# The fourth group's odd half of the out-projection by seven products, in a gated scan with two feed-forward layers

## The chip, the cores and the metric

One core of a Trainium2 chip runs the whole program. The metric is the device time of one execution in microseconds (us). The engines are TensorE (PE in the profile), VectorE (DVE), ScalarE (ACT), GpSimd (POOL) and SyncE (SP), whose queue issues the DMAs. Products on TensorE go to PSUM banks; all else lies in SBUF or in DRAM.

## The reference, cut to what matters

```python
f = lower_bound + (1.0 - lower_bound) * sigmoid(f_logit)      # 6080 x 256
h = f[t] * h + (1.0 - f[t]) * x[t]                            # for t in range(6080)
h1 = y @ moe_w_in;   g1 = maximum(0.01 * h1, h1);             x2 = g1 @ moe_w_out
h2 = x2 @ moe2_w_in; g2 = where(h2 > 0, h2, exp(minimum(h2, 0)) - 1)
return g2 @ moe2_w_out                                        # 6080 x 256, w_in 256 x 2048
```

A scan over 6080 tokens gives `y` (one row `h` per token), and two feed-forward layers of width 2048 follow, the first with a leaky gate, the second with an exponential one.

## The kernel before, in words

**Tiling.** The tokens are cut into 12 chunks: 512, then 448, then ten of 512. The width 2048 is cut into four groups (q = 0 to 3) of 512. `stream` (from line 292) lists the work as 96 triples (layer, chunk, group): layer 1's chunks 0 and 1 alternate inside each group, then chunks 2 to 11 follow with four groups each, then layer 2's twelve chunks. Each triple has an inward part (256 inputs to 512 hidden values) and an outward part (back to 256 outputs, summed over the four groups of a chunk in PSUM).

**Three matmuls a product.** Numbers are kept as a high and a low part that TensorE can take. `mm3` (line 672; its matmuls are L678, L679 and L680) multiplies high by high, high by low and low by high, in pieces of 256 columns, or of 448 in the short chunk.

**Seven products.** From chunk 2 on, the inward part splits both matrices in two by two blocks and does seven products instead of eight (`product` in `group`), with sums and differences of blocks made beforehand: of the chunk by `operands` (L511, L517, L524), of the weights by `combine` (L328). The outward part has an even half (rows E) and an odd half (rows O) of the gate's values. The even half is always plain: `straight`. The odd half is plain as well, or goes by seven products where `seven(l, c, q)` says so; the table `SEVEN` (line 215) holds that for each layer and group as a range of chunks. For such a group `odd_operands` (line 956) makes the differences on VectorE (L969 one of 512 columns, L966 two of 256), casts to a high part on ScalarE (L980: 768 and 1024 columns) and makes the low part on VectorE (L983, the same sizes), into two operand tiles, `aB` and `aT`. A plain half has one cast (L857) and one low part (L861) of 1024 columns. Out of the seven products three go straight to banks 1 and 0 of the chunk (`some(gates["B"], ...)`), and four (`some(gates["T"], ...)`, the group's last) to bank 0 and to two extra banks, `s` and `z`. At the end of a chunk `leave` (line 991) copies `s` and `z` out with ScalarE (L1029), adds them up on VectorE (L1031, L1032, L1036) and adds the sums to banks 1 and 0 (L1033, L1041).

**Weights.** `weights` (line 362) decodes one unit of weights on VectorE and ScalarE (L416, L419, L422, L425, L429) and splits it in high and low. Units that go by seven products (`sums`) are stored as seven blocks. In layer 1 such an odd unit first stays plain, and `finish` (line 338; L349, L328, L355, L357) turns it into seven blocks after the last chunk that uses it plain. The sixteen units of layer 2 are prepared while layer 1 runs, one about every two groups from the 17th triple on, are stored in DRAM (`w2d`) and fetched by `reload` (line 461) when layer 1 needs its weights no more. Where a group of layer 2 goes back to plain, `back` loads the one block that the plain form needs again.

**What sets the order.** All operations are first collected by a planner (`Plan`): each has an engine, a cost in us, a due time, operations that it comes after, and tiles that it takes and gives from pools (seven PSUM banks and one seed bank, six operand tiles, five `h`, three `ws`, and so on). `emit` then fills the engines' queues: of the operations that could start, that with the lowest rank is next, where a rank is the due time of the users less the costs on the way. Each engine runs its queue in order. `SHIFT` holds for each kind of group a string of letters that move ranks by steps of a quarter of a us (N is none). So `SHIFT`, and the costs, change only the order of the instructions and which tile each takes.

Of the kernel before, what the change touches and what calls it, by code (L numbers as in the profile page):

```python
# [15 lines left out]
ALU = mybir.AluOpType  # L16
P = 128
SHIFT = {
    (1, 'x', 0): 'NNNNNNNNNNNNNNNNN7',
    (1, 'w', 'I2'): 'NrNNBN?',  # L20
    (1, 'w', 'O2'): 'NNiUXe',
    (1, 'w', 'E0'): 'NMNNNm',
    (1, 'x', 1): 'NNNNi.9NNNNNNONFNNNkg4',
    (1, 0, 'first1'): 'N*NNNNNNNNNNNNNNNNNNNNN*',
    (1, 1, 'first0'): 'NNNNN*NNNNNN7',
    (1, 1, 'first1'): 'NNNNNNNNNNNNNNNNNNNNN4',
    (1, 'f', 'I'): 'N_eNPbANX',
    (1, 2, 'first0'): 'NNNNNNNNNNNNNNNN2',
    (1, 2, 'first1'): '*',
    (1, 'w', 'O0'): 'NNN1Nir',  # L30
    (1, 3, 'first0'): 'NNNNNNNNNNNN^NN*NNNNNNNNr',
    (1, 3, 'first1'): 'NNNNNNNNNNNNfJNNNNNNNNN;NNNc',
    (1, 'x', 2): 'NNNNANNNNN5UV8NNNNN*NNNN\\NNr@N`=Na*SKNq',
    (1, 0, False): 'NNNNNNNNNNNNNNNNNa6',
    (1, 1, False): 'NNN-NNNN5NNNNNNNaNMN*',
    (1, 'f', 'O'): 'NNNNN8I',
    (1, 2, False): 'NNNNNNNNlNNNNNNNNf',
    (1, 3, False): 'NNN3NENNLNNNN6:YN+RNNNNNN/NNNNNNNN6',
    (1, 0, True): 'N>NNNHNNKNNNNN?NNVNkNNNNNNNNN1',
    (1, 1, True): 'NNNNNNNNNNUNNDNNAN2KBNNNrN1NN5',  # L40
    (1, 2, True): 'NNNNNNNNNN>NNNlNNNNNcNN1R',
    (2, 'w', 'I2'): '-rcNNZH01r=N+_NI',
    (2, 'w', 'O2'): 'NNNNNNNN*NNNNNNr',
    (2, 'w', 'E0'): 'N]NENp',
    (2, 'x'): 'NNNNNNNYR',
    (2, 0, True): 'NWNLNMNNNN*NNJN5NNa[<L>lNN:NNKNNNNNA',
    (2, 1, True): 'NNNrNNNNNNNNNNENNNNNNN<TN>NNEP',
    (2, 2, True): 'NNNNNNNN<NNNN*T=NNNNRMBgIiNNELNNNNN*',
    (2, 3, False): 'NNN<NNNNNN;NNN2NNS5ENN1rNNNNNNNNNNNN7NNN\\NNNN8NNNB',
    (2, 0, 'last'): 'NNNANNNNNNNNN<=5NNNNSNNNNNNNNN+',  # L50
    (2, 1, 'last'): 'NNNNNNNNFNNNNNNNNNNNNNNNNNNNN/',
    (2, 2, 'last'): 'NN,NNNNNNNNNNNNYN:HiYN/',
    (2, 3, 'last'): 'NNNNNNNNNNNNNNCSNnNNNNNXQ5NNNNNNNNNNNNNNNNNNN<',
}


# [103 lines left out]
def kernel(  # L160
# [51 lines left out]


    SI, SO = 7 * P, 2 * D
    SEVEN = {(1, 0): range(3, 12), (1, 1): range(3, 12), (1, 2): range(3, 12), (2, 0): range(0, 11), (2, 1): range(0, 11), (2, 2): range(0, 11)}

    def sums(l, u):

# [39 lines left out]
    def v2(n):  # L258
        return 0.07 + n / 1920.0

    def s1(n):
        return 0.09 + n / 1200.0

    def mm(n):
        return max(0.111, n * 0.000444)
# [8 lines left out]
    def dve(*a, **k):  # L274
        return plan.add("DVE", *a, **k)
# [86 lines left out]
    def weights(l, u, due, gate=()):  # L362
# [46 lines left out]
        def val():  # L409
# [6 lines left out]
        up = dve(v2(n), None, lambda: nc.vector.tensor_scalar(  # L416
            out=tile_("up"), in0=top(), scalar1=0x7F, scalar2=None, op0=ALU.bitwise_and,
        ), [ld], take=[(b, "up", "up")])
        sg = dve(v2(n) + 0.05, None, lambda: nc.vector.tensor_scalar(  # L419
            out=fr(), in0=top().bitcast(I8), scalar1=2.0, scalar2=-2.0, op0=ALU.min, op1=ALU.max,  # L420
        ), [ld], take=[(b, "wf", "ws")])
        ex = act(s1(n) + 0.1, None, lambda: nc.scalar.activation(  # L422
# [156 lines left out]
    def gated(c, natural, gates, hold):  # L579
# [8 lines left out]
        for k in range(KD):  # L588
# [6 lines left out]
            for nm, src in (("f", f2), ("x", x2)):  # L595
                if natural:
                    def load(nm=nm, src=src, k=k, b=b):
                        nc.sync.dma_start(
                            out=b["r" + nm][2][:pb, : n // pb * P].rearrange("p (b d) -> p b d", d=P),
                            in_=src[t0 : t0 + n, k * P : (k + 1) * P].rearrange("(b p) d -> p b d", p=pb),  # L600
                        )

                    ld = dma(0.75 if c == 0 and k else 0.9, (-200.0 + 4 * k if nm == "f" else -199.0 + 5 * k) if c == 0 else None, load, gates[:1], take=[(b, "r" + nm, "raw")], late=3.1)

                    def turn(nm=nm, b=b, k=k):
                        for i in range(n // pb):
# [80 lines left out]
    def group(i):  # L687
# [36 lines left out]
            return o  # L724

        def snap(name, bank, after):
            return act(s1(2 * h), None, lambda: nc.scalar.copy(out=ps(name), in_=ps(bank)), after, take=[(b, name, "sn")])  # L727

        def add(name, s, bank, sn, after, **k):
            return dve(v1(2 * h), None, lambda: nc.vector.tensor_tensor(  # L730
# [30 lines left out]
            gO, gE = "hO", "hE"  # L761
        else:
            pX = product("X", A11, B11, True, False, [], take=[(b, "X", "bank"), (b, "R", "bank")])
            z1 = act(s1(2 * h), None, lambda: nc.scalar.copy(out=ps("Y"), in_=ps("X")), [pX], take=[(b, "Y", "seed")])
# [12 lines left out]
            if final:  # L777
                pass
            elif l == 1:
                a, o = (act(s1(2 * h), None, lambda s=s, name=name: nc.scalar.activation(  # L780
                    out=half("hO", s), in_=two(ps(name)), func=AF.Prelu, alpha=0.01), [done],
                    take=[(b, "hO", "h")], give=[(b, name, home)])
                    for s, name, done, home in ((1, "Y", C11, "seed"), (0, "X", pX, "bank")))
# [3 lines left out]
                gO, gE = "hO", "hE"  # L787
            else:

                a, o = (act(s1(2 * h), None, lambda s=s, name=name: nc.scalar.activation(  # L790
                    out=half("eO", s), in_=two(ps(name)), func=AF.Relu, scale=-1.0), [done],
                    take=[(b, "eO", "ws")])
                    for s, name, done in ((1, "Y", C11), (0, "X", pX)))
# [197 lines left out]
    def leave(l, c, i, yb, swapped):  # L991
# [30 lines left out]
        if "s" in last:  # L1022
# [3 lines left out]
            def at(s, e=None):  # L1026
                return sb["sb"][2][:, s * h : (e or s + 1) * h]

            cps = [act(s1(n), soon, lambda s=s, k=k: nc.scalar.copy(out=at(s, s + 2), in_=yb[k][2][:, :n]), [last[k]],  # L1029
                       take=[(sb, "sb", "h")], give=[(yb, k, "bank")]) for s, k in ((0, "s"), (2, "z"))]  # L1030
            u2 = dve(v1(h), soon, lambda: nc.vector.tensor_tensor(out=at(2), in0=at(2), in1=at(1), op=ALU.add), cps)  # L1031
            u4 = dve(v1(h), soon, lambda: nc.vector.tensor_tensor(out=at(0), in0=at(0), in1=at(2), op=ALU.add), [u2])  # L1032
# [19 lines left out]
            return  # L1052
        for k in (1, 0):
            tb = {}
            tr = dve(v1(n), None, lambda tb=tb, k=k: nc.vector.transpose(
                out=tb["o"][2][:, :n], in_=(ob[k]["o"] if done else yb[k])[2][:, :n]),
                [done.get(k), last[k]], take=[(tb, "o", "t")], give=[(ob[k], "o", pool_) if done else (yb, k, "bank")])
            sent = []
# [89 lines left out]
```

## Time and profile before

| | us |
|---|---|
| median of 3 runs | 981.82 (981.72 to 981.86) |
| the profiled execution | 981.77 |
| its span, first to last instruction | 979.7 |
| ScalarE busy | 812.8 (83 % of the span) |
| GpSimd busy | 14.8 (2 %) |
| TensorE's granted clock | 1.000 of full speed, mean |

The busy time of an engine is the time in which an instruction of it was recorded; matmuls are pipelined and their ends are modelled. The share of the chain that ended last is 97 % TensorE, 1 % VectorE, and under half a per cent for ScalarE and for DMAs.

### The profile page before, as it was taken

To read this page: it belongs to the slowest core of one execution; us is meant where nothing else is said; L and a number is where in the kernel's file an instruction comes from. 1 tells how busy PE (TensorE), PEld (TensorE's weight loads), DVE (VectorE), ACT (ScalarE), POOL (GpSimd) and SP (SyncE) were. 2 spreads that over 40 slices of the span, in tenths; PEclk is the share of its full clock that TensorE was granted. 3 is DMA by queue.
4 is the path that set the end of the run, shared out by engine and by line. 5 is a ranking of instruction groups with operands and counts; after the bars stand their busy time and mean duration, and the time that the engine had idled before them with its cause. 6 is when DMAs were issued, how large, how long until landed. Compare 5 with 4: busy or idle time off the path is not lost.

```text
span 979.7 us, 20612 instructions
## 1 busy us (share of the span) xinstructions
PE 972.4 (99%) x8330; PEld 967.0 (99%) x8330; DVE 889.4 (91%) x1376; ACT 812.8 (83%) x1202; POOL 14.8 (2%) x22
## 2 busy tenths in 40 slices
PE   8999999999999999999999999999999999999998
PEld 8999999999999999999999999999999999999998
DVE  7899999999999899897689889999999999999975
ACT  6767787898888979888689798888898888988874
POOL 0000000000000000000000000000000000000000
PEclk9999999999999999999999999999999999999999
DMA  6542314556466465535860101012011020110210
GB/s 197 131 118 56 77 41 114 128 120 160 110 145 132 109 156 128 124 107 166 282 230 30 23 22 42 14 31 40 13 37 23 23 45 11 34 23 22 39 23 22
DMA packets 162702, 81.98 MB, mean 84 GB/s; under 512 B 133808, under 2 KB 148400, under 8 KB 162608
## 3 DMA queue, kind: packets, MB, share of 16 engines
q1 hardware_dynamic: 160032, 74.12, 28.4%
q0 software_dynamic: 2304, 6.55, 4.7%
q8 instruction: 65, 1.06, 0.5%
q14 instruction: 29, 0.24, 0.1%
q10 hardware_dynamic: 272, 0.00, 0.0%
HBM read 48.54 MB, written 32.11 MB: 82 GB/s over the span
## 4 chain that ended last, share of the span: by engine, by line
PE 97%; DVE 1%; DMA 0%; ACT 0%; issue 0%; DVEq 0%
PE bank L679 30%; PE bank L678 30%; PE bank L680 30%; PE bank L903 2%; PE seed L678 2%; PE seed L680 2%; PE seed L679 2%; DMA raw<-in_f_logit_dram 0%; DVE bt L645 0%; DVE ws L425 0%; DVE t L637 0%; DVE ws L429 0%; DVE wI L444 0%; PE bank L607 0%; DVE up L416 0%
## 5 line engine op out<-in xcount | busy, mean ns | idle before, releaser
L679 PE MATMUL bank<-op,wI 128*128 128x256 f32 (+2 forms) x1136 | 316.8, 279 | 0.8 <-DVE op L556 0.8
L678 PE MATMUL bank<-op,wI 128*128 128x256 f32 (+2 forms) x1136 | 316.7, 279 | 0.0
L680 PE MATMUL bank<-op,wI 128*128 128x256 f32 (+2 forms) x1136 | 316.4, 279 | 0.0
L679 PEld LDWEIGHTS bank<-op,wI 128*128 128x128 f32 x1136 | 213.4, 188 | 2.1 <-DVE op L556 1.6
L678 PEld LDWEIGHTS bank<-op,wI 128*128 128x128 f32 x1136 | 213.4, 188 | 1.0 <-DVE h L730 0.2
L680 PEld LDWEIGHTS bank<-op,wI 128*128 128x128 f32 x1136 | 213.4, 188 | 0.6 <-DVE wI L444 0.2
L679 PE MATMUL bank<-op,wE 128*128 128x256 f32 (+1 forms) x704 | 197.2, 280 | 0.0
L678 PE MATMUL bank<-op,wE 128*128 128x256 f32 (+1 forms) x704 | 197.2, 280 | 0.0
L680 PE MATMUL bank<-op,wE 128*128 128x256 f32 (+1 forms) x704 | 197.1, 280 | 0.0
L679 PE MATMUL bank<-op,wO 128*128 128x256 f32 (+2 forms) x656 | 182.9, 279 | 0.0
L678 PE MATMUL bank<-op,wO 128*128 128x256 f32 (+2 forms) x656 | 182.8, 279 | 0.0
L680 PE MATMUL bank<-op,wO 128*128 128x256 f32 (+2 forms) x656 | 182.7, 279 | 0.0
L730 DVE TENSOR_TENSOR h<-bank,sn 128x512 f32<-128x512 f32 (+1 forms) x176 | 119.5, 684 | 28.5 <-PE bank L680 23.8
L680 PEld LDWEIGHTS bank<-op,wE 128*128 128x128 f32 x704 | 132.2, 188 | 0.4
L678 PEld LDWEIGHTS bank<-op,wE 128*128 128x128 f32 x704 | 132.2, 188 | 0.4
L679 PEld LDWEIGHTS bank<-op,wE 128*128 128x128 f32 x704 | 132.2, 188 | 0.3
L678 PEld LDWEIGHTS bank<-op,wO 128*128 128x128 f32 x656 | 123.2, 188 | 0.3
L680 PEld LDWEIGHTS bank<-op,wO 128*128 128x128 f32 x656 | 123.2, 188 | 0.2
L679 PEld LDWEIGHTS bank<-op,wO 128*128 128x128 f32 x656 | 123.2, 188 | 0.2
L727 ACT COPY sn<-bank 128x512 f32<-128x512 f32 (+1 forms) x176 | 102.3, 583 | 10.5 <-PE bank L680 9.7
L983 DVE TENSOR_TENSOR op<-h,op 128x768 fp32r<-128x768 f32 (+2 forms) x87 | 98.1, 1131 | 5.8 <-ACT op L980 5.7
L980 ACT CAST op<-h 128x768 fp32r<-128x768 f32 (+2 forms) x87 | 85.3, 981 | 19.9 <-PE bank L680 18.3
(115 smaller groups left out, 1828.5 us busy)
## 6 DMA issues: line engine op xcount, KB each, us to landing
ws<-in_moe_w_in_dram SPq DMA_DIRECT2D x32, 255.6 KB, 3.7
ws<-in_moe_w_out_dram SPq DMA_DIRECT2D x32, 255.6 KB, 3.5
w2dI<-ws SPq DMA_DIRECT2D x16, 448.0 KB, 2.8
wI<-w2dI SPq DMA_DIRECT2D x8, 896.0 KB, 6.9
y1d<-t SPq DMA_DIRECT2D x22, 256.0 KB, 2.9
bt<-y1d SPq DMA_DIRECT2D x22, 256.0 KB, 2.9
raw<-in_f_logit_dram SPq DMA_DIRECT2D x80, 64.0 KB, 2.9
raw<-in_x_dram SPq DMA_DIRECT2D x80, 64.0 KB, 2.5
```

What stands on the lines that cost most here:

```text
L678: nc.tensor.matmul(ps[:, s], wop[0], a[0][:, s], start=start and z == 0, stop=False, skip_group_check=True)
L679: nc.tensor.matmul(ps[:, s], wop[0], a[1][:, s], start=False, stop=False, skip_group_check=True)
L680: nc.tensor.matmul(ps[:, s], wop[1], a[0][:, s], start=False, stop=stop, skip_group_check=True)
L727: return act(s1(2 * h), None, lambda: nc.scalar.copy(out=ps(name), in_=ps(bank)), after, take=[(b, name, "sn")])
L730: return dve(v1(2 * h), None, lambda: nc.vector.tensor_tensor(out=half(name, s), in0=two(ps(bank)), in1=two(ps(sn)), op=ALU.add), after, **k)
L903: nc.tensor.matmul(dst, ops(part, j, t), wide(z, j), start=s in fresh and t % 2 + j + z == 0, stop=False, skip_group_check=True)
L980: hi = act(s1((e - s) * h), None, lambda s=s, e=e, src=src: nc.scalar.copy(out=part(0, s, e), in_=src()), [*after, *highs[-1:]], take=[(b, ...
L983: lows.append(dve(v1((e - s) * h), None, lambda s=s, e=e, src=src: nc.vector.tensor_tensor(out=part(1, s, e), in0=src(), in1=part(0, s, e) ...
```

## The change

The table `SEVEN` gets two more entries: the fourth group's odd half goes by seven products in layer 1 from chunk 3 on, and in layer 2 in chunks 0 to 5. By `sums` the fourth odd unit is then kept as seven blocks in both layers (its SBUF tile grows from 2 x 512 to 2 x 896 values a partition), layer 1 finishes it after chunk 2, and layer 2 reloads its plain block before chunk 6. Some costs that the planner counts with are set anew: ScalarE's copies out of PSUM 0.03 us less (`s1p`), VectorE's transposes 0.025 more, one decoding step 0.05 less. All strings of `SHIFT` are replaced.

```diff
 SHIFT = {
-    (1, 'x', 0): 'NNNNNNNNNNNNNNNNN7',
...
-    (2, 'w', 'I2'): '-rcNNZH01r=N+_NI',
...
+    (1, 'x', 0): 'NNNNNNNNNNNNNNN8',
...
+    (2, 'w', 'I2'): 'NWNrfgRNF6IN+NNT',
...
-    SEVEN = {(1, 0): range(3, 12), (1, 1): range(3, 12), (1, 2): range(3, 12), (2, 0): range(0, 11), (2, 1): range(0, 11), (2, 2): range(0, 11)}
+    SEVEN = {(1, 0): range(3, 12), (1, 1): range(3, 12), (1, 2): range(3, 12), (1, 3): range(3, 12), (2, 0): range(0, 11), (2, 1): range(0, 11), (2, 2): range(0, 11), (2, 3): range(0, 6)}
...
+    def s1p(n):
+        return 0.06 + n / 1200.0
...
-        sg = dve(v2(n) + 0.05, None, lambda: nc.vector.tensor_scalar(
+        sg = dve(v2(n), None, lambda: nc.vector.tensor_scalar(
...
-                    got[nm] = dve(v1(n), None, lambda nm=nm, tl=tl: nc.vector.transpose(out=tl(nm), in_=tl("r" + nm)),
+                    got[nm] = dve(v1(n) + 0.025, None, lambda nm=nm, tl=tl: nc.vector.transpose(out=tl(nm), in_=tl("r" + nm)),
...
-            return act(s1(2 * h), None, lambda: nc.scalar.copy(out=ps(name), in_=ps(bank)), after, take=[(b, name, "sn")])
+            return act(s1p(2 * h), None, lambda: nc.scalar.copy(out=ps(name), in_=ps(bank)), after, take=[(b, name, "sn")])
```

The other lines that are left out put `s1p` for `s1` at four more copies out of PSUM, and the 0.025 at the transpose of the output.

## Rows read from the trace of the kernel before

**Rows 1.** The page: busy us, share of the span, instructions of an engine

```profile
PE 972.4 (99%) x8330; PEld 967.0 (99%) x8330; DVE 889.4 (91%) x1376; ACT 812.8 (83%) x1202; POOL 14.8 (2%) x22
```

**Rows 2.** TensorE in order of time: start us, us, what

```profile
653.51 0.28 PE L678 MATMUL bank<-op,wO 128*128 128x256 f32 x1
...
654.87 0.28 PE L678 MATMUL bank<-op,wI 128*128 128x256 f32 x1
```

**Rows 3.** Busy time by stretch: stretch, us, busy us and instructions, clock, DMA share, GB/s

```profile
120.00:440.00 320.00, 320.00 (x2826) 320.00 (x2825) 305.59 (x501) 274.55 (x421) 12.36 (x14) 1.00 0.52 121
440.00:520.00 80.00, 80.00 (x709) 80.00 (x708) 63.66 (x92) 63.61 (x93) 1.73 (x2) 1.00 0.63 212
520.00:600.00 80.00, 80.00 (x661) 78.94 (x660) 72.01 (x107) 68.24 (x99) 0.00 (x0) 1.00 0.13 27
644.50:684.30 39.80, 39.80 (x353) 39.80 (x353) 37.55 (x54) 34.88 (x50) 0.00 (x0) 1.00 0.13 28
```

**Rows 4.** TensorE's waits: who waited for whom, us, times, longest us

```profile
PE bank L679 <- DVE op L556: 0.8, 2, 0.5
```

**Rows 5.** TensorE in order of time, in the chunk of 448 tokens

```profile
566.32 0.27 PE L678 MATMUL bank<-op,wO 128*128 128x224 f32 x1
...
567.65 0.29 PE L678 MATMUL bank<-op,wI 128*128 128x256 f32 x1
```

**Rows 6.** VectorE in order of time, in a layer-2 chunk

```profile
657.21 0.69 DVE L969 TENSOR_TENSOR h<-ws 128x512 f32<-128x512 f32 x1
657.81 0.42 DVE L1031 TENSOR_TENSOR h<-h 128x256 f32<-128x256 f32 x1
658.15 0.42 DVE L966 TENSOR_TENSOR h<-ws,h 128x256 f32<-128x256 f32 x1
...
660.50 0.95 DVE L983 TENSOR_TENSOR op<-ws,op 128x768 fp32r<-128x768 f32 x1
661.37 1.22 DVE L983 TENSOR_TENSOR op<-h,op 128x1024 fp32r<-128x1024 f32 x1
```

**Rows 7.** VectorE's groups, 120 to 440 us: busy us, mean ns, idle us before

```profile
L730 DVE TENSOR_TENSOR h<-bank,sn 128x512 f32<-128x512 f32 x65 | 44.5, 686 | 11.7 <-PE bank L680 11.1 <-ACT h L785 0.2
...
L328 DVE TENSOR_TENSOR ws<-ws 128x128 f32<-128x128 f32 x44 | 11.2, 284 | 0.1
...
L425 DVE SCALAR_TENSOR_TENSOR ws<-ws,ws 128x512 int32<-128x512 int32 x15 | 10.2, 682 | 0.0
...
L419 DVE TENSOR_SCALAR ws<-ws 128x512 f32<-128x512 int8 x15 | 6.6, 439 | 0.0
...
L328 DVE TENSOR_TENSOR h<-h 128x128 f32<-128x128 f32 x12 | 3.2, 283 | 0.0
...
L349 DVE TENSOR_TENSOR h<-wO 128x512 f32<-128x512 f32 x3 | 2.0, 665 | 0.0
L357 DVE TENSOR_TENSOR wO<-h,wO 128x384 fp32r<-128x384 f32 x3 | 1.6, 548 | 0.0
L357 DVE TENSOR_TENSOR wO<-h,wO 128x128 fp32r<-128x128 f32 x3 | 0.8, 278 | 0.0
```

**Rows 8.** ScalarE in order of time, in the same layer-2 chunk

```profile
656.23 1.08 ACT L1029 COPY h<-bank 128x512 f32<-128x512 f32 x2
...
658.27 0.84 ACT L980 CAST op<-ws 128x768 fp32r<-128x768 f32 x1
```

**Rows 9.** DMA issues: count, KB each, median us from issue to landing

```profile
wO<-w2dO SPq DMA_DIRECT2D x6, 128.0 KB, 3.9
```

**Rows 10.** TensorE in order of time, where the next chunk's outward products begin

```profile
669.15 0.28 PE L678 MATMUL bank<-op,wO 128*128 128x256 f32 x1
```

**Rows 11.** VectorE's groups in a layer-2 chunk, 644.5 to 684.3 us

```profile
L861 DVE TENSOR_TENSOR op<-ws,op 128x1024 fp32r<-128x1024 f32 x5 | 6.1, 1219 | 0.5 <-ACT op L857 0.5
...
L805 DVE SCALAR_TENSOR_TENSOR ws<-ws,h 128x1024 f32<-128x1024 f32 x4 | 4.9, 1222 | 1.2 <-ACT ws L803 1.2
...
L796 DVE SCALAR_TENSOR_TENSOR ws<-ws,seed 128x512 f32<-128x512 f32 x4 | 2.7, 686 | 0.4 <-ACT ws L794 0.2
```

More of the change, by code (lines that the diff above doesn't have):

```diff
@@ L18 @@
 SHIFT = {
-    (1, 'x', 0): 'NNNNNNNNNNNNNNNNN7',
[L20 to L41, printed above, removed]
-    (2, 'w', 'I2'): '-rcNNZH01r=N+_NI',
@@ L43 @@
[L43 to L52, printed above, removed]
@@ L53 @@
-    (2, 3, 'last'): 'NNNNNNNNNNNNNNCSNnNNNNNXQ5NNNNNNNNNNNNNNNNNNN<',
+    (1, 'x', 0): 'NNNNNNNNNNNNNNN8',
+    (1, 'w', 'I2'): 'Nb',
+    (1, 'w', 'O2'): ':N3NNNNB',
+    (1, 'w', 'E0'): 'NNNNNrS3',
+    (1, 0, 'first0'): 'NNNNNNNNNNNNNBNNN5',
+    (1, 'x', 1): 'NNNNNNN*NNNNN7NNNNZVm',
+    (1, 0, 'first1'): 'NNNNN,NNNNNNT7',
+    (1, 1, 'first0'): 'NNNNNNNNNNNNNNNN*',
+    (1, 1, 'first1'): 'NNNNNNNNNNN+NN@G',
+    (1, 'f', 'I'): 'rINN7FHNJ',
+    (1, 2, 'first0'): 'NNNNNNNNNNNNNNNNNNN*',
+    (1, 3, 'first0'): 'NNNNNNNNNNNNNNN7',
@@ new lines @@
+    (1, 'x', 2): 'NNNNCNNNNNC>1NNNNNNZNNNNN*NN^NNZNNN3NRP',
+    (1, 0, False): 'NNNNNNNNNNNNNFNNNo6NNNNNNN*',
+    (1, 1, False): 'NNNNNNNN:N>NNNNNDNr',
+    (1, 'f', 'O'): 'NNN,9',
+    (1, 2, False): 'NNN3NNNNNNNNNNNNNNN:',
+    (1, 3, False): 'NGNNNNNNNNNNNNNNNN-',
+    (1, 0, True): 'N>NNNHN*NNNNNNNNNPNNZ*N*S,NNNN:',
+    (1, 1, True): 'NNNNNNNNNNNNN1Nq56NBhNNN8NN<',
+    (1, 2, True): 'NNNNNJNNKNNNNNo9HhNgeNNAANNNN<',
+    (1, 3, True): 'NNNNN8NNNNNNN*N8NbNNN=NrZNN7',
+    (2, 'w', 'I2'): 'NWNrfgRNF6IN+NNT',
@@ new lines @@
+    (2, 'w', 'O2'): 'NWNNNNWN;N@NNrNj',
+    (2, 'w', 'E0'): 'Nf;NN`NN9NN:',
+    (2, 'x'): 'NNNNNHNNQ',
+    (2, 0, True): 'NNNgNNNNNNLNNN1NrNV*8IFNNY*NZBN;',
+    (2, 1, True): 'NNNUNKNNNNNNNNNNN>/dNNNNN0NNi;NNNN*',
+    (2, 2, True): 'NNN@NNNNQN@NNNNNNNWNNN?NNXNNJE',
+    (2, 3, True): 'NINNNNNNNN*N/N04H1NVNNXRMQNNQMNNNNNNNNNNN9NNrNNNNNNN*',
+    (2, 3, False): 'NANNNNNN?N/NNNN.N*9N>rNNNN3NNNNNNNN*NNNNNNNNNl',
+    (2, 0, 'last'): 'NFNNNGNNNNNNNNNNNNNk',
+    (2, 2, 'last'): 'NNNBNNNNNN*NNNNNN<C',
@@ L54 @@
+    (2, 3, 'last'): 'NNN?NNNNNNNNNNNNNNNNNNMF9NNNNNNNNNNNNNNNNNNNNNNNN>',
 }
@@ L763, in group @@
             pX = product("X", A11, B11, True, False, [], take=[(b, "X", "bank"), (b, "R", "bank")])
-            z1 = act(s1(2 * h), None, lambda: nc.scalar.copy(out=ps("Y"), in_=ps("X")), [pX], take=[(b, "Y", "seed")])
+            z1 = act(s1p(2 * h), None, lambda: nc.scalar.copy(out=ps("Y"), in_=ps("X")), [pX], take=[(b, "Y", "seed")])
             pR = product("R", S3, T3, True, False, [])
@@ L779, in group @@
             elif l == 1:
-                a, o = (act(s1(2 * h), None, lambda s=s, name=name: nc.scalar.activation(
+                a, o = (act(s1p(2 * h), None, lambda s=s, name=name: nc.scalar.activation(
                     out=half("hO", s), in_=two(ps(name)), func=AF.Prelu, alpha=0.01), [done],
@@ L788, in group @@
             else:
-                a, o = (act(s1(2 * h), None, lambda s=s, name=name: nc.scalar.activation(
+                a, o = (act(s1p(2 * h), None, lambda s=s, name=name: nc.scalar.activation(
                     out=half("eO", s), in_=two(ps(name)), func=AF.Relu, scale=-1.0), [done],
@@ L1027, in at @@
                 return sb["sb"][2][:, s * h : (e or s + 1) * h]
-            cps = [act(s1(n), soon, lambda s=s, k=k: nc.scalar.copy(out=at(s, s + 2), in_=yb[k][2][:, :n]), [last[k]],
+            cps = [act(s1p(n), soon, lambda s=s, k=k: nc.scalar.copy(out=at(s, s + 2), in_=yb[k][2][:, :n]), [last[k]],
                        take=[(sb, "sb", "h")], give=[(yb, k, "bank")]) for s, k in ((0, "s"), (2, "z"))]
@@ L1054, in leave @@
             tb = {}
-            tr = dve(v1(n), None, lambda tb=tb, k=k: nc.vector.transpose(
+            tr = dve(v1(n) + 0.025, None, lambda tb=tb, k=k: nc.vector.transpose(
                 out=tb["o"][2][:, :n], in_=(ob[k]["o"] if done else yb[k])[2][:, :n]),
```

## The prediction

> **What bounds the kernel now.** I read the busy table of the page first, then the waits of TensorE, then busy time by stretch, then one layer-2 chunk instruction by instruction. The table puts TensorE at 972.4 us of a span of 979.7 and VectorE at 889.4 [rows 1]. That busy time is modelled, so the starts have to show whether TensorE has holes. In the steady part each 256-column matmul starts 0.11 us after the one before: twelve of them take the stretch from 653.51 to 654.87, 113.3 ns each [rows 2]. The 320 us from 120 to 440 hold 2826 of them and the next 80 us 709, at 113 ns each, so no hole is left there to close [rows 3]; in the whole list of its waits TensorE waits for VectorE 0.8 us, in a line of the first two chunks [rows 4]. TensorE bounds the kernel by its number of matmuls, and only fewer columns can make it faster. The reader should then look at VectorE, which is close behind: 305.59 us busy of the 320 us from 120 to 440 (layer 1 from about the fourth chunk, while the weights of layer 2 are being prepared), 63.66 of the next 80, 72.01 of the 80 after these, and 37.55 of the 39.80 us of one layer-2 chunk [rows 3].
>
> **What the change removes.** A chunk's fourth group does its odd half with four weight blocks, each on two halves of the chunk by three matmuls: 24 matmuls of 256 columns. Seven products of three matmuls make 21. It saves 3 × 0.1133 = 0.34 us. The edit adds 9 groups of layer 1 (fourth to twelfth chunk) and 6 of layer 2. Of these 15, one is the 448-token chunk of layer 2: there twelve matmuls of 224 columns take 566.32 to 567.65, 0.111 us each, hardly less than 256 columns take, so 21 are 2.33 us [rows 5], against twelve long ones of 448 columns, the same work as 24 of 224. The saving lies between 0 and 0.33 us; I count 0.1, as few long instructions lose less time between them. Sum: 14 × 0.34 + 0.1 = 4.86 us. Nothing else on TensorE is added or removed.
>
> **What it adds on VectorE.** Per changed group: one difference of 512 columns, two of 256, and a low part of 768 + 1024 columns where one of 1024 stood. The prices are start-to-start, because an instruction's record overlaps the next one's: 0.60 us for 512 columns (657.21 to 657.81, recorded 0.69), 0.34 for 256 (657.81 to 658.15, recorded 0.42), 0.87 for 768 (660.50 to 661.37, recorded 0.95) [rows 6]. So 0.60 + 2 × 0.34 + 0.87 = 2.15 us. In a layer-2 chunk that makes 37.55 + 2.15 = 39.70 us of VectorE work in a chunk that should shrink to 39.80 - 0.34 = 39.46 us [rows 3]. VectorE is overdrawn by 0.24 us a chunk, in the five full chunks by 1.2 us together. The 80 us from 520 to 600 have 8 us of idle VectorE, and each chunk from the seventh on has 2.25 us, so a debt of 1.2 us can be borrowed and paid back, if the order fills the idle time that is there now. Bounds for layer 2: 0 (borrowed whole) to 1.2 us lost, as long as no wait is left in the chunk; waits are the slower rival below.
> From 120 to 440 us in layer 1 the sum is worse. Eight groups bring 8 × 2.15 = 17.2 us. The fourth group's odd weights are now also kept as sums: their finishing pass is 0.665 + 4 × 0.283 + 0.548 + 0.278 = 2.6 us by records, 2.1 with the overlap of 0.08 each; the same four combinations for layer 2 add 4 × 0.284, or 0.8 with the overlap [rows 7]. 305.6 + 17.2 + 2.1 + 0.8 = 325.7 us of work, in 320 - 8 × 0.34 = 317.3 us of TensorE time: an overdraft of 8.4 us. What can move is the preparation of layer 2's weights, wanted only when layer 2 begins. Behind 440 us VectorE has 80 - 63.66 = 16.3 us idle, less two more groups (4.3) and the time that these save (0.7), so 11.3 us [rows 3]: room for 8.4. One unit of weights is by records two decodes of 0.44, two passes of 0.68 and, for most units, four combinations of 0.284, 3.4 us, some 2.75 with the overlaps; there are fifteen such in the 320 us, one every 21 us [rows 7]. So three units must slip behind 440 us. Their tiles are used by nothing else in layer 1, so late units stop nobody by themselves. Bounds: 0 lost to 8.4 us lost.
>
> **A rule that speaks against it.** The rows say that VectorE's instructions overlap: a record of 0.69 us, and the next start after 0.60 [rows 6]. The Trainium skill, in "VectorE: DVE Perf Modes", section "The DRAIN you can't avoid", says that the next instruction does not start until the pipe has emptied. By that rule the third rival below would be the forecast. The trace disagrees with it for these instructions, so that rival gets a small chance.
>
> **What it adds elsewhere.** ScalarE gets a cast of 768 columns per group, recorded at 0.84 us [rows 8]; it has 4.9 us idle in a layer-2 chunk (34.88 busy of 39.80) and 45 us in the 320 [rows 3], so I cost it at 0; without that cover it would be 15 × 0.84 = 12.6 us. The reload of the fourth odd unit grows and is split in two, and one more small load puts a plain block back before the seventh chunk; the DMA engines are busy 13 % of a layer-2 chunk [rows 3] and the load has most of a chunk of time: 0, or up to 3.9 us once, what such a small load takes to land now, if it started only when it is wanted [rows 9]. The order table is replaced whole; its entries move ranks both ways, and no time can be read out of them. It can reach the 0.8 us at the start [rows 4], which the edit otherwise leaves alone: -0.8 to +0.8 (as much lost as there is to gain), and I take 0.
> One hand-over changes. The two banks of partial sums (s and z) used to be full after the third group and were copied out during the fourth; now they are full at the chunk's last product. In the chunk read, 1.36 us pass between the end of these products (654.87) and the first copy, and the two copies take 1.08 us [rows 2, 8]; the next chunk's first odd products begin only at 669.15, long after these copies [rows 10], and open three banks. With seven banks, four in the old chunk and two in the running inward products, one is free; the other two come from s and z about 1.4 us after the end, if ScalarE turns to them at once. Two inward products of six matmuls (0.68 us each) between the old chunk's end and the new one's start cover that. Price 0 to 0.68 us a chunk end, one product's time if only one fits; I take 0, since inward products can be put in there.
>
> **The sum.** 981.77 us is the profiled execution (span 979.7 and 2.1 around it), 0.05 under the median of 981.82. With TensorE still without holes: 981.8 - 4.9 = 976.9. I leave 0.9 us in holes, close to the lower bounds (0 of 1.2, 0 of 8.4), since the idle time is there and most of it, 11.7 of the 14.4 us from 120 to 440, lies before one line, the addition that takes a product as TensorE ends it, and there other work can be done [rows 7]. **Forecast 977.7 us**, own range 976.4 to 979.6.
>
> **The rivals.**
> 1. *Layer 1's overdraft lands on TensorE.* If weights units keep their place, operands come late and holes open. Half of 8.4 us is 4.2: 976.9 + 4.2 = 981.1, no change. For it: three units must slip by up to 60 us, and VectorE is 95 % busy all the way to there [rows 3]. Against it: nothing needs them before layer 2. Chance 0.18; it reaches from 979.6 to 983.5.
> 2. *Slower: VectorE's waits stay.* VectorE runs in order, and in a layer-2 chunk it stands 1.2, 0.5 and 0.4 us idle before three lines that take ScalarE's results (the exponential and the casts) [rows 11]. If these 2.1 us can't be filled, a chunk needs 37.55 + 2.15 + 2.1 = 41.8 us against 39.8 now: 2.0 us worse in five chunks, 10 us, and layer 1 gives back 9 × 0.34 = 3.1: 981.8 + 10 - 3.1 = 988.7 with all of them, 984.5 with 60 % of them. It is slower than now from 0.7 us of wait a chunk on (0.1 of room and 3.1 / 5). For it: the margin is negative before any wait is counted. Against it: these waits stand in an order that has 2.25 us a chunk to spare, and other work, the new differences among it, can be put ahead of the waiting lines. Chance 0.11.
> 3. *Bound by VectorE, evenly.* If the added instructions overlap nothing, they cost their records, 0.69 + 2 × 0.42 + 0.95 = 2.48 us a group [rows 6]. A layer-2 chunk is then 37.55 + 2.48 = 40.03 us, 0.23 worse than now, 1.2 us in five, and layer 1's overdraft is 8 × 0.33 = 2.6 us larger, 11.0 of 11.3, so that its gain of 3.1 us goes to holes: 981.8 + 1.2 = 983.0. Against it: the starts above. Chance 0.04.
> 4. *The bank hand-over eats the gain.* Half of 0.68 us at 15 chunk ends is 5.1 us: 982.0. Chance 0.05.
> 5. *The change does not do what it says*, because the order table loses at the start or end what the products save: 0.8 us at the start, 977.7 + 0.8 = 978.5; it stays faster. Chance 0.02.
>
> **How the numbers follow.** 0.2 % is 2 us, about what a measurement of this kernel tells from no change: faster is below 979.86, slower above 983.78. Forecast 0.60 and rival 5 are faster, 0.62, with 0.09 of rivals 1 and 4 that lose only part: 0.71. Same: 0.13 of rivals 1 and 4, 0.03 of rival 3: 0.16. Slower: rival 2, 0.11, and 0.02 from the far end of 1 and 3: 0.13. The range 976.3 to 982.3 leaves out a little below the floor of 976.9 (a better start) and the slower cases.
>
> **What would show it.** Right: three matmuls fewer in each of 14 groups, and in the 448-token chunk's fourth group 21 short for 12 long; 113.3 ns still between starts, so that a full chunk of 351 matmuls (168 inward, 183 outward) becomes one of 348; VectorE at or above 98 % from 120 to 440 us and in layer 2's first six chunks, then as before; three or so first passes of weights behind 440 us. Wrong: TensorE waits for VectorE at low or high parts in the list of waits (rivals 1 to 3), or for ScalarE's copies of s and z at the chunk's end (rival 4). If VectorE's idle time stays at 2 us a chunk in the changed groups, rival 2 holds; and if layer 2's chunks still take 39.8 us the forecast fails, whatever the total.

## The result, and the profile after

The changed kernel takes 990.50 us (median of 4 runs, 990.29 to 990.60) against 981.84: 1.0088 times as long, interval 1.0070 to 1.0105. The forecast was 977.7, faster; the time lies outside the range, on the other side. The profiled execution took 990.40 with a span of 988.2. Some executions of five kernels here, the one before among them (1000.17, 999.89), take some 18 us longer than the others: medians are of all executions, ratios and the two times of e6 leave the longer ones out, and the profiles of e6 and e12 are of longer ones.

The page, busy time by engine (the form of [rows 1]):

```profile
PE 980.6 (99%) x8297; PEld 974.9 (99%) x8297; DVE 921.3 (93%) x1447; ACT 825.7 (84%) x1219; POOL 14.7 (1%) x22
```

The edit moves line numbers: L678 to L680 of the kernel before are L680 to L682 here. TensorE has 33 matmuls fewer than in [rows 1]. That is what the edit asks for: 14 groups with 3 fewer, and 21 short ones for 12 long in the chunk of 448 tokens, +9. Still it is busy 8 us longer. The whole list of its waits:

```profile
PE seed L1079 <- POOL ident masks.py:199: 1.4, 1, 1.4
PE bank L609 <- DMA raw<-in_f_logit_dram: 1.0, 1, 1.0
PE seed L682 <- DVE wI L446: 0.6, 1, 0.6
PE bank L609 <- DMA raw<-in_x_dram: 0.4, 1, 0.4
PE bank L681 <- DVE op L558: 0.3, 1, 0.3
```

All five end within the first 60 us; behind these the list is empty. No changed group is in it, neither for operands nor for banks. So fewer matmuls, no holes, and more time: each matmul must take longer. Busy time by stretch, after; the columns are those of [rows 3] (busy time of TensorE, its weight loads, VectorE, ScalarE and GpSimd, then clock, DMA share and GB/s):

```profile
120.00:440.00 320.00, 320.00 (x2826) 320.00 (x2825) 318.58 (x536) 279.01 (x431) 12.30 (x14) 1.00 0.51 119
440.00:520.00 80.00, 80.00 (x709) 80.00 (x708) 70.00 (x107) 66.57 (x95) 1.73 (x2) 1.00 0.66 227
583.60:927.80 344.20, 344.20 (x2924) 344.20 (x2923) 325.20 (x464) 297.78 (x408) 0.00 (x0) 1.00 0.14 28
620.00:740.00 120.00, 120.00 (x1021) 120.00 (x1021) 116.17 (x168) 104.73 (x145) 0.00 (x0) 1.00 0.14 27
```

and one stretch of layer 2 before:

```profile
620.00:740.00 120.00, 120.00 (x1062) 120.00 (x1061) 113.19 (x161) 105.26 (x145) 0.00 (x0) 1.00 0.13 28
```

In layer 1 the number of matmuls in 320 and in 80 us is exactly that of [rows 3]: 113 ns each. In layer 2 the same 120 us hold 1021 where they held 1062, at a granted clock of 1.00 and with TensorE busy throughout in both. From 583.60 to 927.80 us, 2924 matmuls take 344.20 us, 117.7 ns each. TensorE in order of time shows where that begins (start us, us, what) and where it ends:

```profile
583.49 0.27 PE L682 MATMUL bank<-op,wO 128*128 128x224 f32 x1
583.60 0.35 PE L680 MATMUL bank<-op,wI 128*128 128x256 f32 x1
583.78 0.28 PE L681 MATMUL bank<-op,wI 128*128 128x256 f32 x1
583.90 0.28 PE L682 MATMUL bank<-op,wI 128*128 128x256 f32 x1
584.02 0.28 PE L680 MATMUL bank<-op,wI 128*128 128x256 f32 x1
...
927.70 0.28 PE L682 MATMUL bank<-op,wE 128*128 128x256 f32 x1
927.82 0.34 PE L680 MATMUL bank<-op,wI 128*128 128x256 f32 x1
927.99 0.28 PE L681 MATMUL bank<-op,wI 128*128 128x256 f32 x1
...
928.58 0.28 PE L680 MATMUL bank<-op,wE 128*128 128x256 f32 x1
928.69 0.28 PE L681 MATMUL bank<-op,wE 128*128 128x256 f32 x1
928.80 0.28 PE L682 MATMUL bank<-op,wE 128*128 128x256 f32 x1
```

The chunk of 448 tokens now ends with matmuls of 224 columns. The first 256-column one behind it starts at 583.60 and the next only 0.18 us later, a step larger than 0.12, and from there on the starts lie 0.12 us apart. That lasts for more than eight chunks, until another single step of 0.17 us at 927.82; soon after it they lie 0.11 apart again. I call the two the short spacing (113.3 ns) and the long one (117.7).

The step of 0.18 us is a late start: the first inward matmul's weight load comes at 583.56, 0.07 us later than the steps before it would put it, and 0.05 us after ScalarE's copy out of a bank has ended (start us, us, what):

```profile
582.92 0.59 ACT L766 COPY seed<-bank 128x512 f32<-128x512 f32 x1
583.38 0.19 PEld L682 LDWEIGHTS bank<-op,wO 128*128 128x128 f32 x1
583.56 0.19 PEld L680 LDWEIGHTS bank<-op,wI 128*128 128x128 f32 x1
```

So it looks like a short wait for a bank, which the rows don't name. The list of waits can't show it: the matmul recorded at 583.49 lasts 0.27 us, past the late start, so TensorE counts as busy. An empty list means no gap in the records, not that every start was in time.

At 113.3 ns the 2924 matmuls would take 331.3 us, so the long spacing costs 12.9. The account closes: 981.77 - 4.86 + 12.9 = 989.8, and 0.6 is left to the 990.40 measured, of the order of the 0.9 that the prediction had left for holes. Or from the other side: 990.5 - 12.9 = 977.6, the forecast.

### The profile page after: what moved, and what is told of

The parts are those of the page before. It is cut to its first block, busy times and chain, and to the rows that moved or that the text cites. A ratio compares the mean times of both kernels' runs of the same rounds, so it can differ in the third digit from the quotient of the medians.

```text
span 988.2 us, 20647 instructions
## 1 busy us (share of the span) xinstructions
PE 980.6 (99%) x8297; PEld 974.9 (99%) x8297; DVE 921.3 (93%) x1447; ACT 825.7 (84%) x1219; POOL 14.7 (1%) x22
## 4 chain that ended last, share of the span: by engine, by line
PE 96%; DVE 2%; issue 1%; DMA 1%; ACT 0%; SPq 0%; DVEq 0%
PE bank L680 29%; PE bank L681 29%; PE bank L682 29%; PE bank L905 2%; PE seed L680 2%; PE seed L682 2%; PE seed L681 2%; DMA ws<-in_moe_w_in_dram 1%; DVE ws L431 0%; DVE bt L647 0%; DVE ws L427 0%; DVE op L558 0%; DVE up L418 0%; SPq L390 0%; SPq L600 0%
## 5 line engine op out<-in xcount | busy, mean ns | idle before, releaser
L680 PE MATMUL bank<-op,wI 128*128 128x256 f32 (+2 forms) x1136 | 318.7, 281 | 0.1
L682 PE MATMUL bank<-op,wI 128*128 128x256 f32 (+2 forms) x1136 | 318.3, 280 | 0.0
L682 PEld LDWEIGHTS bank<-op,wI 128*128 128x128 f32 x1136 | 215.2, 189 | 0.4
L680 PEld LDWEIGHTS bank<-op,wI 128*128 128x128 f32 x1136 | 213.4, 188 | 1.1 <-ACT seed L766 0.3
L680 PE MATMUL bank<-op,wE 128*128 128x256 f32 (+1 forms) x704 | 198.6, 282 | 0.0
L682 PE MATMUL bank<-op,wE 128*128 128x256 f32 (+1 forms) x704 | 198.4, 282 | 0.0
L680 PE MATMUL bank<-op,wO 128*128 128x256 f32 (+2 forms) x645 | 180.7, 280 | 0.0
L681 PE MATMUL bank<-op,wO 128*128 128x256 f32 (+2 forms) x645 | 180.7, 280 | 0.0
L682 PE MATMUL bank<-op,wO 128*128 128x256 f32 (+2 forms) x645 | 180.6, 280 | 0.0
L682 PEld LDWEIGHTS bank<-op,wE 128*128 128x128 f32 x704 | 133.3, 189 | 0.5
L680 PEld LDWEIGHTS bank<-op,wE 128*128 128x128 f32 x704 | 132.2, 188 | 0.4
L985 DVE TENSOR_TENSOR op<-h,op 128x768 fp32r<-128x768 f32 (+2 forms) x111 | 124.4, 1122 | 0.1
L982 ACT CAST op<-h 128x768 fp32r<-128x768 f32 (+2 forms) x111 | 108.9, 981 | 16.5 <-PE bank L682 11.1
L682 PEld LDWEIGHTS bank<-op,wO 128*128 128x128 f32 x645 | 122.3, 190 | 0.2
L680 PEld LDWEIGHTS bank<-op,wO 128*128 128x128 f32 x645 | 121.2, 188 | 0.4
L681 PEld LDWEIGHTS bank<-op,wO 128*128 128x128 f32 x645 | 121.2, 188 | 0.3
```

What stands on the lines that cost most here:

```text
L680: nc.tensor.matmul(ps[:, s], wop[0], a[0][:, s], start=start and z == 0, stop=False, skip_group_check=True)
L681: nc.tensor.matmul(ps[:, s], wop[0], a[1][:, s], start=False, stop=False, skip_group_check=True)
L682: nc.tensor.matmul(ps[:, s], wop[1], a[0][:, s], start=False, stop=stop, skip_group_check=True)
L982: hi = act(s1((e - s) * h), None, lambda s=s, e=e, src=src: nc.scalar.copy(out=part(0, s, e), in_=src()), [*after, *highs[-1:]], take=[(b, ...
L985: lows.append(dve(v1((e - s) * h), None, lambda s=s, e=e, src=src: nc.vector.tensor_tensor(out=part(1, s, e), in0=src(), in1=part(0, s, e) ...
```

## The experiments

Theory A: the spacing is a state of the matmul stream, set by how it is disturbed (a gap, other widths) and kept until the next disturbance; the change's only fault is to leave layer 2 in the long one. Rivals: B, VectorE's or ScalarE's heavier load slows TensorE's reads; C, the new blocks or places of the tiles do it. All edits named "extra matmul" put matmuls into bank X at one place (e12 at two) in front of a product that then overwrites it; they change no result and not the planner's order.

**e1_wide.** The change, and one matmul of 448 columns early in layer 2:

```diff
         def product(bank, s, t, start, stop, after, **k):
             def run():
+                if start and bank == "X" and (l, c, q) == (2, 2, 3):
+                    nc.tensor.matmul(ps("X")[:, :448], wop(("I", pairs[0]), s)[0], src["pb"][2][:, :448], start=True, stop=False, skip_group_check=True)
```

> The change, with one extra matmul of 448 columns on TensorE in layer 2's third chunk (ahead of its fourth group's first product, into a bank that this product overwrites), at about 594 us, when the stream has been at 117.7 ns a matmul for 10 us. Theory A, the pace: TensorE has two steady spacings for this stream of 256-column matmuls, 113.3 and 117.7 ns, and stays in the one it has fallen into until something else runs in between; in the kernel before, every run of 448 columns is followed by 113 ns. Then the spacing falls to 113.3 ns from about 594 us to the end of layer 2's eleventh chunk: 333 us / 117.7 x 4.33 = 12.2 us less, 990.5 + 0.2 - 12.2 = 978.5. Theory B, the load: the spacing is longer because VectorE and ScalarE are busier beside TensorE in layer 2: 990.7. Theory C, the layout: the longer tile of the fourth odd weights moved the addresses of what lies behind it: 990.7.

978.47 us, 0.9964 of before (0.9952 to 0.9977): faster than both kernels, for one matmul *more*. TensorE around it, in order of time:

```profile
590.49 0.28 PE L682 MATMUL bank<-op,wE 128*128 128x256 f32 x1
590.61 0.37 PE L721 MATMUL bank<-op,wI 128*128 128x448 f32 x1
590.81 0.28 PE L680 MATMUL bank<-op,wI 128*128 128x256 f32 x1
590.93 0.28 PE L681 MATMUL bank<-op,wI 128*128 128x256 f32 x1
591.04 0.28 PE L682 MATMUL bank<-op,wI 128*128 128x256 f32 x1
```

Busy time by stretch, e1_wide: one changed full chunk, and the 120 us shown above:

```profile
640.16:679.60 39.44, 39.44 (x351) 39.44 (x350) 39.12 (x58) 35.40 (x50) 0.00 (x0) 1.00 0.14 28
620.00:740.00 120.00, 120.00 (x1061) 120.00 (x1061) 119.02 (x174) 107.84 (x150) 0.00 (x0) 1.00 0.14 29
```

Steps of 0.11 and 0.12 us follow, and 1061 matmuls in the 120 us. Here VectorE is busy 99 % of the stretch, more than in the changed kernel, and TensorE runs at the short spacing: B falls, and C too, since every tile lies where it lay.

**e2_wide_last.** The chunk of 448 tokens does its even half (long matmuls) last:

```diff
-            straight("aE", "E", 0)
-            straight("aE", "E", 1)
+            wide_last = (l, c, q) == (2, 1, 3)
+            if not wide_last:
+                straight("aE", "E", 0)
+                straight("aE", "E", 1)
             some(gates["T"], (M7, S3, T3), (M6, S2, T2), (M5, S1, T1), (C21, A22, T4), give=[(b, "aT", "op")])
+            if wide_last:
+                straight("aE", "E", 0)
+                straight("aE", "E", 1)
```

> The change, with the same instructions, but in the short chunk's fourth group of layer 2 the even half (448 columns a matmul) is done after the four last odd products (224 columns), so that the short chunk ends in long matmuls as it did in the kernel before. Theory A (two paces): the stream of 256 columns behind it starts at 113.3 ns and stays there: 990.5 - 12.7 = 977.8, give or take 1 us for the order around it. Theories B (load) and C (layout): 117.7 ns from there on as before, 990.5 give or take 1.

1003.30 us, 1.0217 (1.0202 to 1.0231). The planner answered the moved operations with another order for all that follows, and TensorE got waits that neither kernel has; the largest of its waits (us in total, times, longest us):

```profile
PE bank L680 <- DVE h L732: 3.7, 6, 1.2
PE bank L680 <- ACT op L859: 2.6, 2, 1.3
PE bank L681 <- DVE op L863: 2.5, 4, 0.9
```

Behind the chunk the spacing is short (113.4 ns from 584.59 to 600.80 us), as A expects, but behind the holes it is now short, now long. As a test of A it is inconclusive, and it shows what an order made for other operations costs.

**e3_order_only.** The new order and costs with the old table:

```diff
-    SEVEN = {..., (1, 3): range(3, 12), ..., (2, 3): range(0, 6)}
+    SEVEN = {(1, 0): range(3, 12), (1, 1): range(3, 12), (1, 2): range(3, 12), (2, 0): range(0, 11), (2, 1): range(0, 11), (2, 2): range(0, 11)}
```

> The kernel before with the changed kernel's order table and planner costs, but its own table of seven products: the new order alone. The strings were made for other groups, so TensorE may get holes. Theory A: the short chunk ends in 448 columns again, so 113.3 ns in layer 2 and 982 to 986. Theory B and C: 113.3 ns too, as neither load nor layout is changed: 982 to 986. It prices the order by itself: if it shows 117.7 ns, the order alone can do it, and B and C fall.

1014.59 us, 1.0356 (1.0311 to 1.0401). Of the 31 us that its profiled execution is longer, 14 are idle TensorE (21.4 us of its span against 7.3); the rest is longer busy time. And it has the long spacing at a place where the kernel before never has it, in layer 1. Busy time from 475 to 520 us, and TensorE in order of time where the long spacing begins, e3_order_only:

```profile
475.00:520.00 45.00, 45.00 (x385) 45.00 (x384) 34.67 (x50) 35.11 (x50) 0.00 (x0) 1.00 0.66 238
```

```profile
467.72 0.28 PE L682 MATMUL bank<-op,wE 128*128 128x256 f32 x1
467.83 0.34 PE L680 MATMUL bank<-op,wI 128*128 128x256 f32 x1
468.01 0.28 PE L681 MATMUL bank<-op,wI 128*128 128x256 f32 x1
468.13 0.28 PE L682 MATMUL bank<-op,wI 128*128 128x256 f32 x1
```

385 matmuls where the kernel before has 400, with none of the added products, none of the larger tiles and a VectorE that is 77 % busy: B falls a second time, and so does C as far as the larger tiles go (the new order can give an operation another tile). The long spacing begins at a single step of 0.18 us, as in the changed kernel, but here no matmul of another width stands near: between 106.69 and 526.19 us all have 256 columns. So a late start can do it alone. It need not: the step of 0.17 us at 152.11 leaves the short spacing.

**e4_products_only.** The new table with the old order:

```diff
 SHIFT = {
-    (1, 'x', 0): 'NNNNNNNNNNNNNNN8',
+    (1, 'x', 0): 'NNNNNNNNNNNNNNNNN7',
...
```

> The fifteen more groups by seven products with the order table and the costs of the kernel before, of which the fourth group's strings do not fit. Theory A: either spacing is possible in layer 2, as the short chunk's end again is 224 columns; 978 to 984 with holes if 113.3 ns, 990 to 996 if 117.7. Theories B and C: 117.7 ns in layer 2's full chunks, at least in the first six (B) or all (C): 986 to 996. If layer 1 alone shows holes in which TensorE waits for VectorE, the new order is what hides VectorE's overdraft.

1026.46 us, 1.0454 (1.0440 to 1.0469). The largest of TensorE's waits in it:

```profile
PE bank L679 <- DVE op L861: 12.5, 16, 1.2
```

With the old order and costs the products cost 45 us, and the new ones take 36 of them back (1026.46 to 990.50). Of the 43 us that the profiled execution is longer, 25 are idle TensorE (32.4 us of its span against 7.3), waits for VectorE and ScalarE above all; the rest is longer busy time, with the long spacing in many stretches.

**e5_wide_late.** The one matmul of e1 at (2, 7, 0), at 763.86 us:

```diff
+                if start and bank == "X" and (l, c, q) == (2, 7, 0):
...
```

> The change with the one extra matmul of 448 columns later: in layer 2's eighth chunk, first group, at about 765 us, half-way through the slow stretch. Theory A (two spacings, the last one is kept until something else runs): 117.7 ns up to 765 us and 113.3 behind it, so about half of the 12.2 us that the early one gave back: (928 - 765) / 117.7 x 4.33 = 6.0, so 990.5 + 0.2 - 6.0 = 984.7. If the early one had helped by moving something else (an address, an order, a wait at the third chunk): 990.7.

984.82 us, 1.0032 (1.0020 to 1.0044). Busy time before and behind the matmul, e5_wide_late:

```profile
620.00:740.00 120.00, 120.00 (x1021) 120.00 (x1021) 116.19 (x168) 104.72 (x145) 0.00 (x0) 1.00 0.14 27
790.00:910.00 120.00, 120.00 (x1061) 120.00 (x1060) 113.13 (x162) 105.56 (x146) 0.00 (x0) 1.00 0.13 27
```

The long spacing stays for the 173 us later that the release comes (6.4 us by 3.7 % of them; 984.82 - 978.47 = 6.35). The same kind of stream runs at either spacing, on either side of one matmul.

**e6_same_width.** The extra matmul at e1's place with 256 columns:

```diff
+                    nc.tensor.matmul(ps("X")[:, :256], wop(("I", pairs[0]), s)[0], src["pb"][2][:, :256], start=True, stop=False, skip_group_check=True)
```

> The change with one extra matmul of 256 columns, the width that the stream has anyway, at the place of the first experiment (about 590 us). Theory A as I have it (a wider matmul lets the next weight load get ahead, a matmul of the same width changes nothing): spacing stays at 117.7 ns, 990.6. If any extra instruction at this place is enough: 978.4.

990.48 and 990.65 us in two executions, 1.0089 (1.0069 to 1.0110): it releases nothing. In the trace the starts behind it (609.43 us) go on 0.12 us apart. So at this place an added instruction is not enough; one of 448 columns is. Busy time in layer 1, e6_same_width:

```profile
120.00:440.00 320.00, 320.00 (x2720) 320.00 (x2719) 310.21 (x515) 271.36 (x415) 11.58 (x13) 1.00 0.51 117
```

2720 in place of 2826: in this execution (1009.33 us) the long spacing holds in layer 1 as well, from about 30 to 538 us. There some 4000 steps behind 256-column matmuls are 4.4 ns longer each, 18 us together. The instructions up to there are those of the changed kernel, whose trace has the short spacing: the same stream can start in either.

**e7_before_wide.** The control: the kernel *before*, with e1's matmul.

```diff
+                if start and bank == "X" and (l, c, q) == (2, 2, 3):
+                    nc.tensor.matmul(ps("X")[:, :448], ...)
```

> A control: the kernel before with the same extra matmul of 448 columns at the same place (layer 2's third chunk, fourth group). Theory A: the spacing is 113.3 ns there already, so only the matmul's own 0.2 us are added: 982.1. If the extra matmul gains something else by itself: below 981.

995.79 us, 1.0143 (1.0128 to 1.0158): a miss, and the most useful one. TensorE around it in e7_before_wide, and its busy time in layer 2:

```profile
591.71 0.28 PE L680 MATMUL bank<-op,wI 128*128 128x256 f32 x1
591.82 0.36 PE L720 MATMUL bank<-op,wI 128*128 128x448 f32 x1
592.02 0.28 PE L678 MATMUL bank<-op,wI 128*128 128x256 f32 x1
592.14 0.28 PE L679 MATMUL bank<-op,wI 128*128 128x256 f32 x1
592.26 0.28 PE L680 MATMUL bank<-op,wI 128*128 128x256 f32 x1
```

```profile
620.00:740.00 120.00, 120.00 (x1021) 120.00 (x1021) 109.02 (x153) 101.36 (x139) 0.00 (x0) 1.00 0.13 28
```

The matmul that releases the changed kernel puts the one before into the long spacing: 14 us lost without any part of the change. That the spacing is a state is confirmed; that a wide matmul always ends it is not.

**e8_before_short.** The kernel before, with twelve extra matmuls of 224 columns:

```diff
+                    for _ in range(12):
+                        nc.tensor.matmul(ps("X")[:, :224], wop(("I", pairs[0]), s)[0], src["pb"][2][:, :224], start=True, stop=False, skip_group_check=True)
```

> The kernel before with twelve extra matmuls of 224 columns at that place, as many as the changed kernel has there when its short chunk ends in seven products; nothing of the change is in it. Theory A: in the changed kernel's trace 8 of 10 runs of 224 columns are followed by 117.7 ns, in the trace of before none of 5; if the stream falls into it, it stays there to the last chunk, 345 us / 113.3 x 4.33 = 13.2 us: 981.9 + 1.3 + 13.2 = 996.4. If it does not fall: 983.2. Theories B (load) and C (layout) have 983.2 for certain.

997.14 us, 1.0157 (1.0140 to 1.0174): the twelve instructions cost 1.3 us, the long spacing behind them the other 14 (1021 matmuls from 620 to 740 us). Twelve matmuls of the width with which the changed kernel ends its short chunk bring the long spacing into the kernel before as well, here with no late start behind them (592.05 to 593.38 us, then 0.12 us a step).

**e9_wide_three, e10_before_three, e11_before_two.** How many wide matmuls set which spacing? Three in the changed kernel and in the one before (two by the high part of the weights, one by the low), and two, both by the high part, in the one before. The "reset" theory: a whole product of three, like the real wide ones, always leaves the short spacing. The "toggle" theory: each wide one swaps.

```diff
+                    for z in (0, 0, 1):      # e9 and e10;   e11: for _ in range(2), with [0] for [z]
+                        nc.tensor.matmul(ps("X")[:, :448], wop(("I", pairs[0]), s)[z], src["pb"][2][:, :448], start=True, stop=False, skip_group_check=True)
```

> The change with three extra matmuls of 448 columns (high, high and low weights, as a whole product of the short chunk has them) where the first experiment had one. Open is what picks the spacing behind a disturbance. Reset: in six traces all runs of 448 columns that are whole products are followed by 113 ns, so three reset the stream: 990.5 + 0.6 - 12.2 = 978.9. Toggle: each wide matmul swaps the spacing, as the single one did in three kernels (slow to fast twice, fast to slow once), so three swap it as one does: 978.9 too. New draw: either 978.9 or 991.1.

> The kernel before with the same three extra matmuls of 448 columns at the same place. Reset (a whole wide product always leads to 113.3 ns): 981.8 + 0.6 = 982.4. Toggle (each wide matmul swaps): 117.7 ns from there on, 995.8 + 0.4 = 996.2. New draw: one of the two.

> The kernel before with two extra matmuls of 448 columns at the same place, where one gave 995.8. Toggle: swapped twice, so 113.3 ns again: 982.2. Reset by whole products only, or a new draw: no certain value, 982.2 or 996.0.

991.73 us, 1.0098 (1.0080 to 1.0117); 982.36, 1.0005 (0.9995 to 1.0015); 982.26, 1.0005 (0.9995 to 1.0014). With three the changed kernel stays long and the one before short, and with two the one before stays short too. Reset falls by e9. Toggle holds for one and for two, but falls by e9 and e10, where three keep what was there.

Reset had a case against it before these runs, in the kernel before itself, which e1's and e9's expectations missed. Behind nine matmuls of 448 columns, three whole products, twelve of 256 run at the long spacing, from 564.90 us to the line at 566.32 with which [rows 5] begins:

```profile
564.70 0.36 PE L680 MATMUL bank<-op,wE 128*128 128x448 f32 x1
564.90 0.28 PE L678 MATMUL bank<-op,wI 128*128 128x256 f32 x1
565.02 0.28 PE L679 MATMUL bank<-op,wI 128*128 128x256 f32 x1
...
566.20 0.28 PE L680 MATMUL bank<-op,wI 128*128 128x256 f32 x1
```

**e12_wide_twice.** The change, with a single wide matmul at (2, 2, 3) and another at (2, 7, 0):

```diff
+                if start and bank == "X" and (l, c, q) in ((2, 2, 3), (2, 7, 0)):
```

> The change with the single extra matmul of 448 columns at both places: at 590 us (as in the first experiment) and in the eighth chunk. Toggle: the first one swaps to 113.3 ns, the second one back to 117.7 for the last 160 us: 978.5 + 0.2 + 6.0 = 984.7. If a wide matmul only ever releases the stream to 113.3 ns: 978.7 (but then the kernel before with one should not have lost 14 us).

984.32 us, 1.0025 (1.0015 to 1.0035). Busy time behind the first and behind the second, e12_wide_twice:

```profile
620.00:740.00 120.00, 120.00 (x1061) 120.00 (x1060) 118.94 (x174) 107.81 (x151) 0.00 (x0) 1.00 0.15 30
790.00:910.00 120.00, 120.00 (x1021) 120.00 (x1021) 109.82 (x155) 101.55 (x140) 0.00 (x0) 1.00 0.13 27
```

The first releases, the second locks again, at the place where e5's released. A single wide matmul swapped the spacing in all five cases (e1, e5, e7, and twice in e12). What a disturbance leaves behind in general stays **open**: no rule that I formed covers one, three and twelve matmuls alike, nor the late starts (e3's at 467.83 us ends in the long spacing, e12's of 0.20 us at 939.40 leaves the long one, the changed kernel's at 927.82 ends it). What in the changed kernel's short chunk ends in the long spacing, and in the kernel before's not, is open with it. Two things changed there, the twelve matmuls of 224 columns and the late start behind them; e8 shows that the first can do it alone, e3 the second, and no run separates them at 583.60 us. Behind runs of 224 columns with at least nine of 256 after them, the first six steps or so are uneven (0.11 to 0.13 us); then 3 of 10 in the changed kernel settle at the long spacing (522.34, 532.34 and 583.60 us), the other 7, and all 9 in the kernel before, at the short one. By this count the 8 of 10 in e8's expectation don't hold.

## Why the prediction was wrong

**The step that failed** is the first line of the sum: "With TensorE still without holes: 981.8 - 4.9 = 976.9". TensorE stayed without holes, but the sum takes for granted that all other matmuls keep their 113.3 ns ("113.3 ns still between starts" was given as what would show it right). They took 117.7 from 583.60 to 927.80 us, 12.9 us more. I had read the spacing in one place [rows 2] and by count in others [rows 3], and took a value that was the same in all of these for a constant of the instruction. The kernel before has the long one too, in the twelve matmuls up to 566.32 us shown at e9, just ahead of the rows that I read [rows 5]. [rows 5] themselves held a hint that I passed over: twelve 224-column matmuls at 0.111 us each, 2 % less for 12 % fewer columns. I used it as a price and did not ask what it leaves behind; e8 shows twelve of that width, put into the kernel before, followed by the long spacing.

The sum has small slips besides: 976.9 + 0.9 is 977.8, and the range stands there twice, as 976.4 to 979.6 and as 976.3 to 982.3. Neither bears on the miss.

**What the change removes: right.** 33 matmuls fewer, and at the short spacing a changed full chunk takes 39.44 us (e1_wide) where it took 39.78 (the distance of the same two lines, one chunk on, in the kernel before): the 0.34 counted.

**VectorE in layer 2: the overdraft wasn't there.** Counted were 37.55 + 2.15 = 39.70 us in a chunk of 39.46. The same instructions show 39.63 us, 2.08 a group, where a chunk takes 40.99 us in the changed kernel, but 39.12 of 39.44, 1.57 a group, in e1_wide:

```profile
640.16:681.15 40.99, 40.99 (x350) 40.99 (x349) 39.63 (x58) 35.90 (x49) 0.00 (x0) 1.00 0.14 27
```

So the price was near what the longer chunk shows, but it does not add up to an overdraft: with less idle time between them, more of the records lie on top of each other (they add up to 43.8 and 43.6 us in the two), and the busy time shrinks.

**VectorE in layer 1: +20.1 was forecast for the 320 us, 13.0 came** (318.58 against 305.59 [rows 3]). Seven changed groups fall into the stretch, not eight (the low parts of plain halves go from 42 to 35): 7 x 1.57 + 2.1 + 0.8 = 13.9, less two additions of 0.60 that moved out (65 [rows 7] to 63) = 12.7. That three units of weights slip behind 440 us was wrong: one first pass lies there in both kernels. It cost TensorE nothing all the same. The rows of VectorE's groups from 120 to 440 us (mean ns, idle us before), after, from which these counts are:

```profile
L732 DVE TENSOR_TENSOR h<-bank,sn 128x512 f32<-128x512 f32 x63 | 42.8, 682 | 0.5 <-ACT t L635 0.3
L863 DVE TENSOR_TENSOR op<-h,op 128x1024 fp32r<-128x1024 f32 x35 | 42.5, 1214 | 0.1
```

The first is the addition before which 11.7 us of idle time lay [rows 7]; 0.5 is left. That this idle time can be filled was right.

**The hand-over of s and z, the loads, ScalarE: right, at 0.** The list of TensorE's waits is empty there. The late start at 583.60 us looks like a bank wait of 0.07 us, though behind another copy than those of s and z.

**The order table: right in the size at the start** (the 0.8 us of [rows 4] became 0.3 and 0.6). What it was there for shows in e4.

**Rivals 1 to 4** fall with the list of waits, and rival 5 with the waits at the start: the slower side came, but not by the mechanism that I put there (rival 2, VectorE's waits, 984.5 to 988.7). The chance for it was 0.11 plus far ends, for reasons that did not act. A rival was missing that was about the price of the bounding engine's own instruction.

## What to carry to other kernels

When one engine is 99 % busy, the time is its number of instructions times their spacing, so check the spacing by count of starts in every stage before and after, not the busy share, which was 99 % for 113 and for 118 ns alike. If an edit that saves work comes out slower with no new wait in the list, look for the place where the spacing changes and at the instruction just there (another width, or a start some 0.07 us late, which the list can't show); one dummy instruction behind that place is a cheap test, and here the remedy: 978.47 us in place of 990.50. Run such a remedy on the old kernel too, since here it made that one 14 us slower.

## What the runs showed of the hardware

A stream of 256-column matmuls, each with its own weight load, has two steady spacings here, 113.3 and 117.7 ns, both at a granted clock of 1.00 (the 2.4 GHz level) and both with TensorE recorded as busy throughout. It stays in the one that it fell into for long: in the long one for the 344 us and 2924 matmuls shown, and in e7 from 592.02 to about 965 us. VectorE's load doesn't decide which: 91 % busy at the long one (e7), 99 % at the short (e1). It changed at a single matmul of 448 columns (five of five, in both directions), not at one of 256 (e6) and not at three of 448 (e9, e10); twelve of 224 were followed by the long one in e8 and in the changed kernel at 583.60 us, elsewhere not always. In a stream of 256 columns alone, single steps of 0.17 to 0.20 us changed it in either direction (e3 at 467.83 us, the changed kernel at 927.82) or left it (e3 at 152.11, e12 at 939.40). The Trainium skill, in "TensorE: Matmul & The Clock Gate", section "Back-to-back issue gap", says that in a stream of weight loads and matmuls both set the spacing, and gives one spacing for a width. That the columns alone don't set it fits the traces, where 224 take 0.111 us and 256 take 0.113 [rows 2, 5]; but they show two spacings for the same pair of instructions, 3.9 % apart.
